# A retention and bilinear-FFN kernel on one core: small filler products at the start, and one pair's stretch moved by four products

## The chip, the cores and the metric

The kernel runs on one core of a Trainium2 chip. The metric is the time of one execution on the device, in microseconds (us). Lower is better. Before the change the median of 7 runs is 329.95 us, with runs from 329.38 to 330.68 us.

The engines are named as in the profile: PE multiplies matrices (PEld is its weight load), DVE and ACT work on vectors, POOL is the general one, and SP issues DMAs. A product is one matrix multiplication instruction. Each is preceded by a weight load of its own, which is an instruction too.

## The reference

There are two layers, the first feeding the second. `q`, `k` and `v` have 8 batches, 8 heads, 576 positions and 64 features; 4608 tokens in all.

```python
def _attn_ref(q, k, v):
    scale = 1.0 / np.sqrt(D_)
    scores = scale * np.matmul(q, k.transpose(0, 1, 3, 2))
    gamma = 1.0 - 2.0 ** (-5.0 - np.arange(H, dtype=np.float32))
    rel = pos[:, None] - pos[None, :]
    Dmat = np.where(rel >= 0, gamma[:, None, None] ** rel[None, :, :], 0.0)
    ret = scores * Dmat[None, :, :, :]
    return np.matmul(ret, v).astype(np.float32)

def _moe_ref(x, w_a, w_b, w_out):      # x is 4608 x 512
    a = x @ w_a                        # 512 x 1536
    b = x @ w_b                        # 512 x 1536
    return (a * b @ w_out).astype(np.float32)
```

The output has 4608 x 512 numbers in float32. The kernel multiplies in bf16.

## The kernel before

**The bulk of the work.** The second layer is computed in blocks of tokens: 512, 256, 256, and then 512 each (`ffn_block`). In a block there are 12 groups F of 128 columns. For each, four products make `pa` (line 728) and four make `pb` (line 743). ACT casts `pa` to `ha` (line 736), and DVE multiplies `ha` with `pb` into `hT` (line 748). After the 12 groups each 128 tokens get 12 products `po` (line 762), which are copied to `osb` and stored. The tiles `pa`, `pb`, `po`, and others of the first layer share four PSUM buffers (`ps_ffn`, tag `ab`).

**The first layer.** Retention is computed in chunks of 64 positions with a running state. The first 768 tokens are done in small steps at the beginning and inside the first block (`score_step`, `state_step`, `output_step`). From token 768 on the tokens are taken in pairs of 128, numbered n (pair 3 is the first, `FIRST`). A pair's work on PE consists of products of 64 x 64 x 64, a quarter of the array each:

- `from_states` (line 613): up to 32 products of states and queries, into `o`;
- `keyed` (line 530): 32 products of keys and values, into `kv`;
- `matched` (line 587): 32 products of keys and queries, into `sc`;
- `from_keys` (line 626): 32 products of scores and values, added into `o`.

`stretch(into, outof)` issues `from_states` for pair `outof`, `keyed` and `matched` for pair `into`, and `from_keys` for `outof`, one after the other. With all four parts it is 128 products and 128 weight loads, hence 256 instructions of PE. Where a state is known to be zero some products are left out: the stretch for pairs 5 and 4 has 240 instructions.

**What follows a stretch on the other engines.** The stretch appends small pieces of work to a list, `later`. One piece is taken off (`pop`) after each `hT`, and at some other points. For pair 5 the six pieces are: two times two sums of `kv` (DVE, line 550); two scalings of `o` into the next block's `xT` (DVE, line 636); then `convert` with the first half of the masked scores; and `convert_swapped` with the second half. `convert` is two casts by ACT (lines 557 and 561), `convert_swapped` two casts by ACT (line 554). These casts make the states which `from_states` of the same pair loads.

**Order.** The order on each engine is written by hand. `ffn_block` yields after every product with that product's cost (1 for 512 columns, 0.5 for 256). The loop at the end adds the costs up. When the sum reaches the place of the first entry of `todo`, and the work is at an edge between groups, that entry runs. `open_alone(5)` at 266 flushes what is left in `later` and issues `from_states` of pair 5; `close_outputs(5)` at 270 issues its `from_keys`. The third block, of 256 tokens, begins at 216, so each of its groups F costs 4.

**Fillers.** At the start PE has no data yet. `warm(count, n)` issues products of a tile of ones whose results nobody reads. The first call is `warm(8, 512)`. Then come the transposes of the first queries and keys (line 316), which wait for casts by DVE (line 299), and more fillers between the first steps.

## Time and profile before

| What | us |
|---|---|
| Median of 7 runs | 329.95 |
| The profiled execution's own time | 329.64 |
| Its span, first to last instruction | 327.9 |
| PE busy with products | 318.0 |
| PEld busy | 168.8 |
| DVE busy | 162.4 |
| ACT busy | 129.2 |
| POOL busy | 114.8 |
| Idle time of PE that the profile puts to no releaser ("issue") before `po`, in 9 places | 1.7 |
| The same before `pa`, in 6 places | 1.0 |

PE's products: 475 recorded for `pb` with 111.2 us, 451 for `pa` with 106.7 us, 429 for `po` with 94.8 us. Some product records are missing, so the counts are slightly under those of the program (3658 products in all, 3621 recorded).

How to read it: times in the timeline are us from the first instruction. A line gives the start, the time covered, the engine, the line of the kernel, the operation with its tiles, and how many instructions are merged (x). In brackets stands the idle time of that engine just before, and what ended it. "issue" means that nothing in the profile explains it. The end of a product is modelled: products overlap, and a single one of 512 columns is shown with 0.38 us, though one follows the other after 0.216 us. So a short idle time in brackets on PE isn't by itself lost time, and like has to be compared with like.

The page also lists DMA queues. Queue 8 is of the kind "instruction": it fetches the program itself. Queue 1 carries the kernel's loads, stores and transposes that SP issues, queue 0 the weight loads that POOL issues.

### The profile page before, as it was taken

To read this page: it belongs to the slowest core of one execution; us is meant where nothing else is said; L and a number is where in the kernel's file an instruction comes from. 1 tells how busy PE (TensorE), PEld (TensorE's weight loads), DVE (VectorE), ACT (ScalarE), POOL (GpSimd) and SP (SyncE) were. 2 spreads that over 40 slices of the span, in tenths; PEclk is the share of its full clock that TensorE was granted. 3 is DMA by queue.
4 is the path that set the end of the run, shared out by engine and by line. 5 is a ranking of instruction groups with operands and counts; after the bars stand their busy time and mean duration, and the time that the engine had idled before them with its cause. 6 is when DMAs were issued, how large, how long until landed. Compare 5 with 4: busy or idle time off the path is not lost.

```text
span 327.9 us, 8698 instructions
## 1 busy us (share of the span) xinstructions
PE 318.0 (97%) x3621; PEld 168.8 (51%) x3658; DVE 162.4 (50%) x291; ACT 129.2 (39%) x277; POOL 114.8 (35%) x146
## 2 busy tenths in 40 slices
PE   7999999999999999999999999999999999999995
PEld 3764467868544554545454545454445444444443
DVE  5744445666536673845274626562556245314421
ACT  6835743553445424533244324442333233213321
POOL 3870069820957067455074205270520000000000
PEclk9999999999999999999999999999999999999999
DMA  7999999999999999994799068935750510031013
GB/s 210 253 186 207 254 231 223 189 216 205 218 220 227 177 212 235 220 217 105 171 216 194 34 159 193 199 97 138 166 115 24 139 35 0 2 96 34 1 32 96
DMA packets 143175, 50.37 MB, mean 154 GB/s; under 512 B 124576, under 2 KB 138656, under 8 KB 143136
## 3 DMA queue, kind: packets, MB, share of 16 engines
q1 hardware_dynamic: 138384, 45.10, 64.6%
q0 software_dynamic: 4752, 4.72, 8.9%
q8 instruction: 28, 0.46, 0.6%
q14 instruction: 11, 0.09, 0.1%
HBM read 37.75 MB, written 9.44 MB: 144 GB/s over the span
## 4 chain that ended last, share of the span: by engine, by line
PE 94%; issue 1%; DMA 1%; DVE 1%; ACT 1%; SPq 0%; ACTq 0%; DVEq 0%
PE pb L743 28%; PE po L762 28%; PE pa L728 27%; PE o L613 2%; PE o L626 2%; DMA vf<-in_v_dram 1%; PE sc L587 1%; PE kv L530 1%; PE kv L360 1%; PE tp L316 1%; PE pa L705 1%; PE o L421 1%; PE sc L331 1%; PE w L792 0%; PE o L405 0%
## 5 line engine op out<-in xcount | busy, mean ns | idle before, releaser
L748 DVE TENSOR_TENSOR hT<-ha,pb 128x512 bf16<-128x512 bf16 (+1 forms) x120 | 75.9, 634 | 98.8 <-PE pb L743 93.3
L736 ACT CAST ha<-pa 128x512 bf16<-128x512 f32 (+1 forms) x120 | 64.9, 544 | 120.1 <-PE pa L728 115.1
L743 PE MATMUL pb<-xT,wb_sb 128*128 128x512 bf16 (+1 forms) x475 | 111.2, 357 | 0.4
L728 PE MATMUL pa<-xT,wa_sb 128*128 128x512 bf16 (+1 forms) x451 | 106.7, 356 | 1.5 <-issue 1.0
L762 PE MATMUL po<-wo_sb,hT 128*128 128x512 bf16 (+1 forms) x429 | 94.8, 373 | 2.1 <-issue 1.7
L743 PEld LDWEIGHTS <-wb_sb 128*128 128x128 bf16 x480 | 47.0, 98 | 46.5 <-issue 0.3
L728 PEld LDWEIGHTS <-wa_sb 128*128 128x128 bf16 x468 | 44.9, 98 | 44.2 <-issue 0.2
L762 PEld LDWEIGHTS <-hT 128*128 128x128 bf16 x444 | 42.3, 98 | 46.9 <-issue 0.3
L464 POOL CAST qkb<-qf 64x1024 bf16<-64x1024 f32 x15 | 15.5, 1031 | 83.3 <-DMA qf<-in_q_dram 83.2
L469 POOL TENSOR_TENSOR vb<-vf,vs 128x1024 bf16<-128x1024 f32 x15 | 28.5, 1903 | 10.4 <-DMA vf<-in_v_dram 5.1
L779 DVE COPY osb<-po 128x512 f32<-128x512 f32 (+1 forms) x16 | 10.8, 675 | 39.3 <-PE po L762 39.3
L777 ACT COPY osb<-po 128x512 f32<-128x512 f32 x20 | 11.7, 587 | 44.3 <-PE po L762 44.3
L636 DVE TENSOR_TENSOR xT<-o,qs 128x512 bf16<-128x512 f32 x30 | 19.5, 683 | 4.4 <-PE o L626 4.4
L550 DVE TENSOR_TENSOR sums<-kv,sums 128x256 f32<-128x256 f32 x46 | 19.5, 423 | 2.8 <-PE kv L530 0.8
L596 DVE TENSOR_TENSOR sT<-sc,mask 128x512 bf16<-128x512 f32 x30 | 19.6, 683 | 0.0
L468 POOL CAST qkb<-kf 64x512 bf16<-64x512 f32 x30 | 17.6, 616 | 0.8
L468 POOL CAST qkb<-qf 64x512 bf16<-64x512 f32 x30 | 17.7, 616 | 0.6
L464 POOL CAST qkb<-kf 64x1024 bf16<-64x1024 f32 x15 | 15.5, 1037 | 6.5 <-DMA kf<-in_k_dram 6.0
L554 ACT CAST states<-sums 64x512 bf16<-64x512 f32 x26 | 16.1, 618 | 0.3
L299 POOL CAST qkb<-kf 128x512 bf16<-128x512 f32 x5 | 3.1, 616 | 18.7 <-DMA kf<-in_k_dram 18.7
L792 PE MATMUL w<-ones 128*128 128x256 bf16 (+1 forms) x34 | 7.4, 346 | 1.5 <-DVE ones L197 1.5
L653 ACT COPY fence<-o 128x2 f32<-128x2 f32 x15 | 2.4, 161 | 15.8 <-PE o L613 15.8
(83 smaller groups left out, 163.3 us busy)
## 6 DMA issues: line engine op xcount, KB each, us to landing
qf<-in_q_dram SPq DMA_DIRECT2D x32, 256.0 KB, 4.7
kf<-in_k_dram SPq DMA_DIRECT2D x32, 256.0 KB, 5.2
vf<-in_v_dram SPq DMA_DIRECT2D x32, 256.0 KB, 5.1
out_dram<-osb SPq DMA_DIRECT2D x25, 256.0 KB, 2.1
out_dram<-osb SPq DMA_DIRECT2D x22, 128.0 KB, 2.7
wo_sb<-in_moe_w_out_dram POOLq DMA_DIRECT2D x3, 512.0 KB, 16.5
qf<-in_q_dram SPq DMA_DIRECT2D x8, 128.0 KB, 3.3
kf<-in_k_dram SPq DMA_DIRECT2D x8, 128.0 KB, 3.5
```

Of the source, the lines that this page charges most:

```text
L464: nc.gpsimd.tensor_copy(qkb[0:64, w], t[0:64])
L468: nc.gpsimd.tensor_copy(to[:, :, 1 - r], fro[:, :, r])
L469: nc.gpsimd.tensor_tensor(vb.rearrange("p (k h d) -> p k h d", k=2, h=H), vf.rearrange("p (k h d) -> p k h d", k=2, h=H), vs2[:, 2 if n in ...
L550: nc.vector.tensor_tensor(sums[:, i], own, prev, op=ALU.add)
L554: nc.scalar.copy(to(half(1 - r)), fro(half(r)))
L596: nc.vector.tensor_tensor(sT[:, on].rearrange("p c k s -> p (c k) s"), sc[:, on].rearrange("p c k s -> p (c k) s"), mask3.unsqueeze(1).to_ ...
L636: nc.vector.tensor_tensor(x_of(t0, 128).rearrange("p c (a s) -> p c a s", a=2), o[:, :, :, kp].rearrange("p a c s -> p c a s"), qs[:, :, s ...
L728: nc.tensor.matmul(pa[:, 0:n], wa_sb[:, c, fs], xT[:, c], start=(c == 0), stop=(c == NC - 1))
L736: nc.scalar.copy(ha[:, 0:n], pa[:, 0:n])
L743: nc.tensor.matmul(pb[:, 0:n], wb_sb[:, c, fs], xT[:, c], start=(c == 0), stop=(c == NC - 1))
L748: nc.vector.tensor_tensor(hT[:, F, 0:n], has[F][:, 0:n], pb[:, 0:n], op=ALU.mult)
L762: nc.tensor.matmul(po[:, 0:width], hT[:, F, u * 128:(u + 1) * 128], wo_sb[:, F, cols], start=(F == 0), stop=(F == NF - 1))
```

## The change

Two things change. The first `warm(8, 512)` becomes three calls of a new function and `warm(5, 512)`. The new function `warm_quads(16)` issues 16 products of 64 x 64 x 64 on the ones, by turns on the upper left and lower right quarter of the array; each call takes a tile of the four shared PSUM buffers. So three products of 512 columns (6 instructions of PE with their weight loads) are replaced by 48 small ones (96 instructions). The number of PE's instructions in the program goes from 7317 to 7407, counting from the branch at the start on.

In `todo` the stretch for pairs 5 and 4 goes from 236 to 240, one group F further on in the third block. The places of the entries around it stay.

```diff
+    def warm_quads(count):
+
+        w = ps_ffn.tile([128, 512], FP32, tag="ab", name="w4")
+        for i in range(count):
+            r = i % 2
+            nc.tensor.matmul(w[half(r), 0:64], ones[half(r), 0:64],
+                             ones[half(r), 0:64], start=True, stop=True)
+
     W1, W2 = 128 * WCOLS[0], 128 * (WCOLS[0] + WCOLS[1])
     vector, pool_ = nc.vector, nc.gpsimd
-    warm(8, 512)
+    for _ in range(3):
+        warm_quads(16)
+    warm(5, 512)
     make_qs(qs_o, 0, 0, 512)
...
     todo += [(170, stretch, (3, None)), (197, stretch, (4, 3)),
-             (236, stretch, (5, 4)), (266, open_alone, (5,)),
+             (240, stretch, (5, 4)), (266, open_alone, (5,)),
              (270, close_outputs, (5,)), (336, stretch, (6, None)),
```

## Prediction

> **What bounds the kernel now.** I read the page first, for the bound.

> ```profile
> span 327.9 us, 8698 instructions
> PE   7999999999999999999999999999999999999995
> PE 94%; issue 1%; DMA 1%; DVE 1%; ACT 1%; SPq 0%; ACTq 0%; DVEq 0%
> q8 instruction: 28, 0.46, 0.6%
> ```

> PE is 94% of the chain of waits and busy in every slice but the ends. After the opening an idle moment of PE is lost time, and nothing else is. The last line is the resource that the change speaks of: 28 packets of 16 KB on queue 8 carry instructions. Next I searched the timeline of PE for idle moments that no semaphore explains. After each dense stretch of 64x64 products PE shows 0.16 us; one place shows more. First the usual exit, then the odd one:

> ```profile
> 119.31 0.33 PEld L762 LDWEIGHTS <-hT 128*128 128x128 bf16 x3
> 119.55 0.38 PE L762 MATMUL po<-wo_sb,hT 128*128 128x512 bf16 x1 [0.16 <-issue]
> ...
> 149.01 0.33 PEld L762 LDWEIGHTS <-hT 128*128 128x128 bf16 x3 [0.28 <-issue]
> 149.24 0.38 PE L762 MATMUL po<-wo_sb,hT 128*128 128x512 bf16 x1 [0.39 <-issue]
> ```

> The timing: the packets of queue 8 start at 56.49, 63.11 and 83.34 us; by the trace PE executes 1205, 1461 and 2229 (block starts) at 55.47, 62.51 and 83.30. So among 256-column products a fetch starts 0.04 to 1.02 us after PE reaches the boundary that triggers it (mean 0.55). A packet takes 0.9 to 1.5 us, mostly 1.25. The one before the odd place ran from 146.18 to 147.51, and PE went on at 149.01: usable 1.5 us after its end.

> [...] The trace agrees: 28 packets of 16 KB, for 28 boundaries among 7317 instructions. [...] Here the trace's clock record reads full from 4.28 us, 2.8 us after the first product; products before that lie 0.43 us apart, later 0.216.

> **The change part by part.**

> *Quarter-array products.* Three products of 512 columns at the half clock go: 3 x 0.427 = 1.28 us. 48 of 64x64x64 come. At full clock the trace shows such products at 10 ns each where four quadrants alternate (128 in 1.23 us, the stretches) and 24 ns where two column halves share their rows (16 in 0.38 us, L360). Two diagonal quarters lie between; twice that at half clock is 20 to 48 ns, so 1.0 to 2.3 us. I take 1.28, no difference. A longer row is covered: the transposes behind the fillers wait for DVE anyway,

> ```profile
> 5.16 0.40 PE L316 MATMUL tp<-identity,qkb 128*128 128x128 bf16 x4 [0.17 <-DVE qkb L299]
> ```

> and the five remaining products shrink to 0.216 us each once the clock is open. With 2.3 us the fillers end at 5.1 instead of 4.6 us, the second transposes start 0.2 later, and the next wait (0.19 us for ACT's vb before L360 at 7.12) takes that up. Cost 0; at most 0.2.

> *Ninety instructions more in front* (96 less 6). Every boundary falls 90 instructions earlier in the work. The odd stretch then has a boundary 91 ahead of it and one in the middle: -0.23 us. I laid the new boundaries over all dense stretches. Next to the one below, the closest is the stretch at old 4958: boundaries 3 instructions ahead of it and 13 behind. Among 512-column products a fetch starts ahead of PE's arrival (146.18 against 147.52), so its block is usable some 1.5 us after arrival, and there PE needs it only after 0.3 + 1.25 + 0.2 + 1.4 = 3.1 us: no stall. In the opening each block lasts over 6 us.

> The one is pair 5's stretch. It keeps 240 instructions and starts at 1991; boundaries are at 1973 and 2229. So 18 ordinary instructions and 238 of the 240 form one block, and only the last load and product belong to the next.

> ```profile
> 75.88 0.26 PEld L613 LDWEIGHTS <-states 64*64 64x64 bf16 x20 [0.21 <-issue]
> 77.11 0.33 PEld L728 LDWEIGHTS <-wa_sb 128*128 128x128 bf16 x4
> ```

> PE reaches 1973 at 75.57 (now instruction 1883). Fetch starts at 75.57 + 0.55 = 76.1, ends at 77.35, is usable at 78.85; with the ends of the ranges 78.1 to 79.45. The stretch starts 8 products of 256 columns later, 75.88 + 0.87 = 76.75, and its last load comes 1.1 us on, at 77.85. Stall 1.0 us (0.25 to 1.6; 0 if blocks are usable earlier than my one case says). Nothing takes it up: DVE's sums for this pair stand behind the next hT, which needs the next pb, so the 0.6 us that PE then loses over PSUM buffers (78.2 to 79.9) come again.

> *Pair 5's stretch four on* (236 to 240: eight 256-column products, one pa and pb). Left in place it would meet the same boundaries. But the move has its own price: the states for `open_alone(5)`, which stays at 266.

> ```profile
> 81.86 0.37 ACT L736 CAST ha<-pa 128x256 bf16<-128x256 f32 x1 [0.50 <-PE pa L728]
> 82.26 0.41 ACT L557 CAST states<-sums 128x256 bf16<-128x256 f32 x1
> 82.57 0.40 ACT L561 CAST left_states<-sums 128x256 bf16<-128x256 f32 x1
> 82.88 0.36 ACT L736 CAST ha<-pa 128x256 bf16<-128x256 f32 x1
> 83.27 1.25 ACT L554 CAST states<-sums 64x512 bf16<-64x512 f32 x2
> 84.42 0.36 ACT L736 CAST ha<-pa 128x256 bf16<-128x256 f32 x1
> ...
> 84.80 0.44 PE L613 MATMUL o<-qkT,states 64*64 64x64 bf16 x32
> ```

> ACT turns the sums into states as the fifth and sixth things popped after the stretch. It ends at 83.27 + 1.25 = 84.52 and PE loads them at 84.80: 0.28 us in hand. After the move the same pops come one pa and pb later: ACT casts ha at 82.73, and the chain of 2.66 us behind it ends at 85.39. PE's work up to L613 is only reordered, so it is there at 84.80 still, and waits until about 85.44: +0.64 us (0 to 0.7). Behind the waiting load stand all of PE's products; nothing later gives it back. ACT's last ha moves ahead of the states, which helps one hT that is not due. A stall inside the stretch moves both sides and doesn't shorten this wait. SP, POOL and the DMA issues keep their order.

> Sum: 0 - 0.23 + 1.0 + 0.64 = +1.41 us. Against the profiled execution: span 327.9 to 329.3, its time 329.64 to 331.05. The median shown is 329.95, 0.31 above that execution, so 331.4.

> **Rivals.**

> Block in time, states late: if the sequencer runs further ahead than I read, or a block is usable soon after its packet ends, the stall falls away: -0.23 + 0.64 = +0.41, 330.35. For it: my 1.5 us come from one place. Against it: at that place nothing else explains the load.

> Not slower, both covered: if PE also arrives at L613 0.64 us later relative to ACT, or ACT's pops come earlier than I place them, only the 0.23 remains: 329.7. It decides once ACT's chain has 0.64 us of reserve more than the 0.28 seen. ACT's start at 81.86 was set by PE, which speaks against.

> Faster: the opening is fetched late now and earlier afterwards. From 14.4 to 17.5 us the dense steps show ten gaps of 0.09 us; were these fetches, 0.9 us would go, with the 0.23: 328.8. It needs all of them to be fetches. Against it: the same 0.09 stands at nearly every entry of a later stretch.

> Clock late: [...] Fillers would end at 4.9 us, [...] the L360 group ends at about 8.6 instead of 8.1: +0.5, with the rest +1.9, 331.9. Nothing in the trace shows such products at half clock.

> **How the numbers follow.** Stall and states both: 0.50. States alone: 0.22. Neither: 0.11. Opening faster: 0.11. Clock late on top: 0.06. 0.2% of the time, 0.66 us, is about what a measurement here can tell from no change. Slower by more than that are the first and the last case and 0.04 of the second (+0.41, near the bound): 0.60. Same: the rest of the second and the third, 0.29. Faster: the fourth, 0.11. The range takes in both smaller cases and the long end of the stall (1.6 instead of 1.0, with 0.2 in the opening): 329.6 to 332.2. The likeliest case alone, with a stall of 0.25 to 1.6, is 330.6 to 332.0.

> **What would show it.** The gap at 149 falls from 0.39 to 0.16 us. Pair 5's last L626 product comes about 1 us after the others, with no semaphore to name. L613 near 86 us waits for ACT's L554, some 0.6 us. Queue 8 has 29 packets. The first transposes still end by 5.4 us. If pair 5's stretch takes 1.23 us as before, my block timing is wrong; if L613 doesn't wait, my ACT chain is.

## The result, and the profile after

The kernel takes 331.84 us after the change (median of 26 runs, 330.37 to 333.05), against 330.19 before (61 runs, 329.25 to 333.43). The ratio is 1.0045, with a 95% interval of 1.0033 to 1.0058. That is 1.5 us slower (1.1 to 1.9). Medians here and below are of all runs, and ratios leave out the three slowest of quads96, which ran at a granted clock of 0.989 to 0.995. The profiled execution took 331.57 us, with a span of 329.9; before it was 329.64 and 327.9.

The page after the change, first the span, PE's busy tenths over 40 slices, the engines' shares of the chain of waits, and the queue of instructions:

```profile
span 329.9 us, 8790 instructions
PE   7899999999999999999999999999999999999995
PE 92%; DMA 2%; SPq 2%; issue 2%; ACT 1%; DVE 1%; ACTq 0%; DVEq 0%
q8 instruction: 29, 0.48, 0.6%
```

PE is the bound as before, so the 2.0 us of span must be time in which PE stands or runs at the low clock of the opening (0.427 us for a product of 512 columns there, 0.216 later, in the kernel before). Queue 8 carries 29 packets instead of 28, for 7407 instructions of PE instead of 7317. By the weight loads that have begun when each packet starts, its packets start 251 instructions of PE apart on average in both traces. The 256 instructions that I count to a block, and the edges counted with them here and below, are an estimate that these numbers fit. The chain of waits now has DMA and SP at 2% each: its first part runs through loads of q in the opening.

To place the 2.0 us I split the span at the first product of L705, which begins the first block of the second layer, and at the last `po`. I call the stretch between them the body.

| | before | after | difference |
|---|---|---|---|
| Start of the first L705 | 17.51 | 18.43 | +0.92 |
| Body: from there to the start of the last `po` | 306.63 | 307.65 | +1.02 |
| From there to the end | 3.79 | 3.78 | -0.01 |

The table of PE's waits by releaser (in total, times, longest) names three waits of this kernel that the one before does not have:

```profile
PE tp L316 <- ACT qkb L299: 0.6, 1, 0.6
PE o L613 <- ACT states L554: 0.4, 1, 0.4
PE o L626 <- ACT fence L653: 0.3, 1, 0.3
```

The first stands in the opening, the other two in the body. The second was expected. In the timeline (start, time covered, in brackets the idle time before and what ended it):

```profile
85.22 1.25 ACT L554 CAST states<-sums 64x512 bf16<-64x512 f32 x2
...
85.88 0.10 PEld L613 LDWEIGHTS <-states 64*64 64x64 bf16 x1 [0.42 <-DVE hT L748]
86.52 0.33 PEld L613 LDWEIGHTS <-states 64*64 64x64 bf16 x31 [0.53 <-ACT states L554]
86.52 0.44 PE L613 MATMUL o<-qkT,states 64*64 64x64 bf16 x31 [0.42 <-ACT states L554]
```

One load goes through at 85.88, and the other 31 wait until ACT's cast ends. From load to load that is 0.64 us, of which I count 0.61 as lost.

The place where I had put the largest loss shows a small one. These are PE's weight loads at the end of pair 5's stretch and behind it:

```profile
78.52 0.36 PEld L626 LDWEIGHTS <-vb 64*64 64x64 bf16 x32
78.92 0.11 PEld L728 LDWEIGHTS <-wa_sb 128*128 128x128 bf16 x2
79.19 0.20 PEld L728 LDWEIGHTS <-wa_sb 128*128 128x128 bf16 x2 [0.15 <-issue]
```

The stretch itself runs through. Two loads behind it PE stands for 0.15 us with no releaser. The stretch at 150 us, whose exit was late before, now leaves with the usual gap:

```profile
150.66 0.33 PEld L762 LDWEIGHTS <-hT 128*128 128x128 bf16 x3
...
150.89 0.38 PE L762 MATMUL po<-wo_sb,hT 128*128 128x512 bf16 x1 [0.16 <-issue]
```

The third wait is one I had not seen coming. `from_keys` (L626) waits for a tiny copy by ACT, the `fence` of line 653, at 235.65. First the kernel before at the same point of the work, then the kernel after:

```profile
233.71 0.16 ACT L653 COPY fence<-o 128x2 f32<-128x2 f32 x1 [0.66 <-PE o L613]
233.92 0.45 PE L626 MATMUL o<-sT,vb 64*64 64x64 bf16 x32
```

```profile
235.65 0.16 ACT L653 COPY fence<-o 128x2 f32<-128x2 f32 x1 [0.94 <-PE o L613]
235.86 0.45 PE L626 MATMUL o<-sT,vb 64*64 64x64 bf16 x32 [0.34 <-ACT fence L653]
```

ACT was idle in both cases and waited for the same product of PE, but the copy starts 0.28 us later. The first product of L626 starts 0.53 us after the one ahead of it, where it was 0.25 before: 0.28 us lost. The same happens at 120.62, where part of it is hidden: 0.18 us lost.

So the body's difference closes: 0.61 (states) + 0.15 (late block) + 0.28 + 0.18 (fences) - 0.23 (the gap at 149 us) = 0.99, against 1.02 measured.

In the opening, the first transposes of step 3 wait for ACT's cast of q, and that waits for the load. Before:

```profile
12.94 0.62 ACT L299 CAST qkb<-qf 128x512 bf16<-128x512 f32 x1
```

And after, in ACT's and in PE's timeline:

```profile
13.87 0.62 ACT L299 CAST qkb<-qf 128x512 bf16<-128x512 f32 x1 [0.92 <-DMA qf<-in_q_dram]
```

```profile
14.54 0.62 PE L316 MATMUL tp<-identity,qkb 128*128 128x128 bf16 x8 [0.59 <-ACT qkb L299]
```

SP issued that load 0.37 us earlier than before (6.96 instead of 7.33), yet it landed 0.93 later (13.85 instead of 12.92). Whether this belongs to the change or to this one execution is a question for the experiments.

### The profile page after: what moved, and what is told of

The parts are those of the page before. It is cut to its first block, busy times and chain, and to the rows that moved or that the text cites. A ratio compares the mean times of both kernels' runs of the same rounds, so it can differ in the third digit from the quotient of the medians.

```text
span 329.9 us, 8790 instructions
## 1 busy us (share of the span) xinstructions
PE 319.2 (97%) x3665; PEld 170.5 (52%) x3703; DVE 162.4 (49%) x291; ACT 129.4 (39%) x277; POOL 114.8 (35%) x146
## 4 chain that ended last, share of the span: by engine, by line
PE 92%; DMA 2%; SPq 2%; issue 2%; ACT 1%; DVE 1%; ACTq 0%; DVEq 0%
PE pb L743 28%; PE po L762 28%; PE pa L728 27%; DMA qf<-in_q_dram 2%; SPq L153 2%; PE o L613 2%; PE o L626 2%; PE sc L587 1%; PE kv L530 1%; PE pa L705 1%; PE kv L360 1%; PE o L421 1%; PE tp L316 0%; ACT states L554 0%; PE o L405 0%
## 5 line engine op out<-in xcount | busy, mean ns | idle before, releaser
L736 ACT CAST ha<-pa 128x512 bf16<-128x512 f32 (+1 forms) x120 | 64.9, 544 | 120.8 <-PE pa L728 115.9
L728 PE MATMUL pa<-xT,wa_sb 128*128 128x512 bf16 (+1 forms) x451 | 106.9, 356 | 1.5 <-issue 1.0
L762 PE MATMUL po<-wo_sb,hT 128*128 128x512 bf16 (+1 forms) x429 | 94.8, 373 | 1.8 <-issue 1.4
L728 PEld LDWEIGHTS <-wa_sb 128*128 128x128 bf16 x468 | 44.9, 98 | 44.4 <-issue 0.4
L762 PEld LDWEIGHTS <-hT 128*128 128x128 bf16 x444 | 42.3, 98 | 46.7
L554 ACT CAST states<-sums 64x512 bf16<-64x512 f32 x26 | 16.1, 618 | 0.3
L299 POOL CAST qkb<-kf 128x512 bf16<-128x512 f32 x5 | 3.1, 616 | 19.0 <-DMA kf<-in_k_dram 19.0
L339 DVE TENSOR_TENSOR sT<-sc,mask_s 128x1024 bf16<-128x1024 f32 x6 | 7.3, 1222 | 3.1 <-PE sc L331 3.1
L653 ACT COPY fence<-o 128x2 f32<-128x2 f32 x15 | 2.4, 161 | 16.4 <-PE o L613 13.6
```

Of the source, the lines that this page charges most:

```text
L554: nc.scalar.copy(to(half(1 - r)), fro(half(r)))
L728: nc.tensor.matmul(pa[:, 0:n], wa_sb[:, c, fs], xT[:, c], start=(c == 0), stop=(c == NC - 1))
L736: nc.scalar.copy(ha[:, 0:n], pa[:, 0:n])
L762: nc.tensor.matmul(po[:, 0:width], hT[:, F, u * 128:(u + 1) * 128], wo_sb[:, F, cols], start=(F == 0), stop=(F == NF - 1))
```

## The experiments

Twelve kernels ran, each in five rounds beside the kernel before. "Ratio" is to the kernel before on the same chip; 0.001 is 0.33 us. Where a wait for `qkT` (a transposed tile that DMA makes) is given, its size is from start to start: from the last product of L530 to the first of L587, less what the kernel before takes there. The bracket of the same line is 0.1 to 0.2 us smaller, as the modelled end of a product hides a part. Three questions: what does each half of the change do, are the body's rows the right ones, and what in the opening costs time?

### Each half alone: quads_only and move_only

quads_only has the small fillers and leaves the stretch at 236:

```diff
+    for _ in range(3):
+        warm_quads(16)
+    warm(5, 512)
-    warm(8, 512)
```

> The filler part alone: 48 quarter-array products in front, pair 5's stretch back at 236. My theory (states late 0.6 us, blocks of instructions late at pair 5's stretch, minus the gap at 149): the states are in time again, so 0.6 us less than the changed kernel. What is left is the block, 0.15 to 1.0 us, and -0.23: 329.9 to 331.0. Rival (the opening carries the loss: small products keep the clock low until 7.5 us): the whole +1.5 stays, 331.7.

Measured: 331.26 us, ratio 1.0034 (1.0018 to 1.0051), so 1.1 us slower: above my range and below the rival's 331.7. The wait for states and the late fences are absent, and so is the late exit at 149 us. The block behind pair 5's stretch is 0.14 us late, not 1. The body is 307.87, and 1.57 of it is one wait for `qkT`:

```profile
133.37 0.45 PE L587 MATMUL sc<-qkT 64*64 64x64 bf16 x32 [1.40 <-DMA qkT<-qkb]
```

Without it the body would be 306.30, 0.33 less than before: 0.23 of it is the late exit, and smaller steps, none above 0.13, more than make up the 0.14 of the block. So in this half alone the body but for that wait is no slower, and still the kernel is. The time must be ahead of the body or in waits such as this one.

move_only has the old fillers and the stretch at 240:

```diff
-             (236, stretch, (5, 4)), (266, open_alone, (5,)),
+             (240, stretch, (5, 4)), (266, open_alone, (5,)),
```

> The move alone: stretch at 240, the old eight fillers. My theory: L613 waits for ACT's states some 0.6 us near 86 us, the gap of 0.39 at 149 stays, no block of instructions is late: +0.6, 330.8. Rival (opening): no change, 330.2.

Measured: 331.31 us, ratio 1.0022 (1.0007 to 1.0038). The median is 0.5 above my 330.8; the ratio gives 0.7 us where I had 0.6, but of other parts. The wait for states is there (0.61), and both late fences (0.46). So the fences belong to the move, not to the fillers. The exit near 149 us is later than ever, as the program keeps its boundary inside the old stretch:

```profile
150.14 0.98 PEld L762 LDWEIGHTS <-hT 128*128 128x128 bf16 x6 [0.98 <-issue]
150.14 1.25 PE L762 MATMUL po<-wo_sb,hT 128*128 128x512 bf16 x5 [0.87 <-issue]
```

PE is without a weight load for 0.98 us here. The packet of queue 8 ran from 147.33 to 148.64, so the block was usable 1.5 us after its end. The body is 308.63; 0.34 of that is a wait for `qkT` near 67 us.

### The states: after_open270 and move270

`open_alone(5)` and `close_outputs(5)` follow the stretch by four products too, so the distance between the sums and their use is the old one. In after_open270 this is done to the changed kernel, in move270 to move_only:

```diff
-             (240, stretch, (5, 4)), (266, open_alone, (5,)),
-             (270, close_outputs, (5,)), (336, stretch, (6, None)),
+             (240, stretch, (5, 4)), (270, open_alone, (5,)),
+             (274, close_outputs, (5,)), (336, stretch, (6, None)),
```

> The changed kernel with the two entries behind the stretch also moved by four: open_alone(5) at 270, close_outputs(5) at 274. My theory: L613 no longer waits for ACT's states, 0.6 us less than the changed kernel: 331.1. Rival (opening): as the changed kernel, 331.7.

Measured: 330.97 us, ratio 1.0024 (1.0007 to 1.0041), 0.7 us less than the changed kernel by the two ratios, whose intervals overlap. The casts and the load that waited for them, now in order:

```profile
84.22 1.25 ACT L554 CAST states<-sums 64x512 bf16<-64x512 f32 x2
...
85.75 0.33 PEld L613 LDWEIGHTS <-states 64*64 64x64 bf16 x32 [0.42 <-DVE sT L596]
```

The load begins 0.28 us after the casts end, the same reserve as in the kernel before. The fences stay late, and the block at pair 5's stretch 0.13 us. The body is 306.88, against 307.65: 0.77 less, where the states wait was 0.61.

> The old fillers, the stretch at 240, and pair 5's state pass and closing each four products later too (270 and 274). Theory 'two late waits in the body': the 0.6 us that L613 waits for L554's states is gone, the two late fences (near 119 and 235, 0.46 together) stay, and so does the late block at 150 us: 330.6 to 330.9 by median, body about 308.0 less any wait for qkT. Rival, the moved stretch costs something of its own that the trace gives no row: the time stays at move_only's 331.2 to 331.4.

Measured: 330.99 us, ratio 1.0014 (0.9999 to 1.0029). No wait for states. The late fences stay, and the late exit at 150 us too (0.48 instead of 0.23). The body is 307.30. The rows give 306.63 + 0.46 + 0.25 = 307.34, so my 308.0 was too high: it counted a wait for `qkT` that this execution does not have. The median lies between my 330.6 to 330.9 and the rival's 331.2.

### The fences: open270_act2, move_act2 and move270_act2

Why would ACT, idle, start a copy 0.28 us late? The copy is preceded by a wait instruction of its own. In the kernels with the moved stretch, at the two late places, the copy follows that wait by 0.32 us instead of 0.04. The two copies have the numbers 191 and 319 among the instructions that the trace records on ACT: 128 apart. The kernels with the moved stretch have 408 of them, the others 406. If ACT's own instructions come in blocks, which is a guess here, the edge fell between wait and copy. Queue 14, the other queue of instructions, carries packets of 8 KB, half the size of queue 8's; the traces do not say which engine each is for. To test it, two tiny copies on ACT are put ahead of the body:

```diff
     load_pair(FIRST + 2, (Q, K))
+    for _ in range(2):
+        nc.scalar.copy(fence, biasq[:, 0:1].to_broadcast([128, 2]))
```

> The changed kernel with open_alone(5) at 270 and close_outputs(5) at 274, and two tiny copies more on ACT before the second layer begins. In the three moved kernels seen so far ACT's fence copy (L653) comes 0.28 us late at 119-121 and 234-236 us, 128 ACT instructions apart, which costs PE 0.46 in all. Theory: these are boundaries of ACT's own blocks of instructions, which two extra instructions push off the fence: both delays go, 0.4 less than after_open270, 330.6. Rival (the fence is late because the moved stretch changes what ACT does there): both stay, 331.0.

Measured: 331.64 us, ratio 1.0031 (1.0011 to 1.0050). In the trace both fences are on time:

```profile
234.15 0.16 ACT L653 COPY fence<-o 128x2 f32<-128x2 f32 x1 [0.38 <-PE o L613]
234.35 0.45 PE L626 MATMUL o<-sT,vb 64*64 64x64 bf16 x32
```

The body is 306.42, 0.46 less than after_open270's. But the time did not fall: the first L705 is at 18.15 instead of 17.52, and the median is higher than the rival's 331.0. That the delay hangs on the number of ACT's instructions ahead is shown by the trace; that a fetch is behind it fits, but no row names one. The gain in time is not shown.

> The old fillers, the stretch at 240 and two tiny copies on ACT ahead of the body, so that ACT's own blocks of instructions change two instructions earlier in the program. Theory: the fences near 119 and 235 us are no longer late (0.28 each at ACT, 0.46 of PE's time), while the states wait of 0.6 stays: 330.7 to 331.0. Rival, the late fences hide in what PE would have waited anyway: 331.2 to 331.4.

Measured: 330.83 us, ratio 1.0009 (0.9991 to 1.0026). The fences near 120 and 235 us are on time, and the wait for states stays with 0.61. The late exit at 150 us is gone as well, which I had not expected: PE came to that place later, and goes on at 150.66 after 0.17 us with no releaser. A wait for `qkT` (0.8 us) took its place.

> The old fillers, the stretch at 240, the state pass and the closing at 270 and 274, and the two tiny copies on ACT. Theory: both costs of the move in the body are gone and the time is before's but for the late block at 150 us (0.5 more than before's at 149): 330.3 to 330.8, with no wait of L613 for L554 and no late fence. Rival, the move has a cost that neither row holds: above 331.0.

Measured: 331.00 us, ratio 1.0018 (1.0000 to 1.0036), above my 330.8 and just at the edge of the rival. The trace has no wait for states, no late fence and no late exit. The body is 306.42, 0.21 less than before. All of this profile's loss lies ahead of it: the first L705 is at 19.29, and most of that is one wait, listed by releaser as

```profile
PE kv L360 <- ACT vb L307: 0.9, 1, 0.9
```

which again ends with a load that came late. So in this execution the body's costs are those in the rows, and the move has no other there.

### The small products, or the place of the blocks? n128, full90, merge16, quads_late, quads96

n128 cuts the eight first fillers into 32 full-array products of 128 columns, 48 instructions more, with the stretch at 236:

```diff
-    warm(8, 512)
+    warm(32, 128)
```

> No small products: the first eight fillers of 512 columns become 32 of 128 columns on the whole array, 48 instructions more, stretch at 236. Block boundaries lie clear of all stretches, the gap at 149 is gone. Theory O: the clock opens at 4.3 to 5 us as before, nothing is lost in the opening: 330.0 to 330.2. Rival (any rise of the number of instructions in front costs in the opening): 330.7 or more.

Measured: 330.14 us, ratio 0.9993 (0.9978 to 1.0007). The late exit at 149 us is gone, the body is 306.77 with two waits for `qkT`, 0.66 together. Here more instructions in front cost nothing.

merge16 goes the other way: four later groups `warm(4, 256)` become `warm(2, 512)`, 16 instructions fewer.

> The kernel before with fewer instructions instead of more: four groups of four fillers of 256 columns become two of 512 each, 16 instructions less, stretch at 236. The block boundary that lay at the end of the stretch at 149 us moves 16 instructions on. Theory: gap at 149 falls from 0.39 to 0.16, nothing else moves: 330.0 to 330.3. Rival (the gap belongs to that stretch, not to the boundary): 0.39 stays.

Measured: 330.54 us, ratio 1.0007 (0.9984 to 1.0029), above my 330.3 by median but no change by ratio. The exit that was late is on time (149.03 follows 148.63 directly), and the body is 306.42. A boundary 16 instructions later does as well as one 90 earlier: the gap moves with the boundary. In exchange PE stands for 0.46 us in the opening at 16.34, with no releaser, 1.4 us after the first packet of queue 8 ended (13.76 + 1.14).

quads_late keeps the first fillers and puts 52 small products in place of seven later ones, 90 instructions more:

```diff
-    warm(5, 256)
+    warm_quads(22, 2, 256)
...
-    warm(4, 256)
+    warm_quads(30)
```

> The same 90 instructions more, but after the clock is open: the eight fillers of 512 columns stay, and seven later fillers of 256 columns become 52 quarter-array products (22 in place of three before the second score step's successor, 30 in place of four before the transposes of step 3). Stretch at 236. My theory: as quads_only, since the block boundaries are the same: 329.9 to 331.0. Rival (opening): the clock opens at 4.3 us as before, and the time is that of the kernel before or 0.2 better: 330.0 to 330.2.

Measured: 331.66 us, ratio 1.0040 (1.0022 to 1.0058), above my range and the rival's. The opening has a stall of this kind too, larger:

```profile
15.39 0.25 PE L421 MATMUL o<-sT,vb 64*64 64x128 bf16 x4 [0.81 <-issue]
```

0.97 us are lost there, and 0.40 behind pair 5's stretch. The first packet ended at 13.82, 1.6 us before PE went on.

quads96 has twice the small products (96 for six of 512 columns), 180 instructions more.

> The filler part doubled, stretch at 236: 96 quarter-array products for six of the eight. 180 instructions more, which puts no block boundary just ahead of any stretch, so no block of instructions is late in the body and the gap at 149 is gone (-0.23). Theory O (small products don't count for the clock; [...] and the opening pays): first score step later than with 48 (after 7 us), time 0.5 or more above quads_only: 331.5 to 332.5. Rival B (the filler part costs through late blocks at pair 5's stretch): 329.9 to 330.2.

Measured: 331.99 us, ratio 1.0043 (1.0019 to 1.0066). The record of PE's clock reads full from 4.4 us, as in the kernel before, so small products do not keep the clock from opening. The second score step begins at 10.07, where it was 10.08. So the time lies in theory O's range by luck: what O said of the clock did not happen. In its profile `qkT` costs 2.6 us at 70.89 and 0.3 more later, and the first L705 starts at 18.63.

full90 takes up what n128 left open. It has exactly the 90 more instructions of the change, all full-array, in the opening:

```diff
-    warm(8, 512)
+    warm(32, 128)
...
-    warm(4, 256)
+    warm(8, 128)
...
-    warm(3, 256)
+    warm(6, 128)
...
-    warm(5, 256)
+    warm(10, 128)
```

(and two more groups of four, and one of one, cut in the same way).

> No quarter-array products and the stretch at 236, but exactly the 90 more PE instructions that the change adds, all as full-array products (the eight openers as 32 of 128 columns, and six later filler groups cut into twice as many products of 128 columns), so the block boundaries of the body stand where they stand with the quads in front and the stretch at 236 (331.26). Theory B, the extra cost of the quads alone comes from where the block boundaries and the fetches fall, in the opening among others: 330.9 to 331.4, first L705 at 18.2 or later or a fetch before 11 us with a step's load behind it landing late. Theory Q, it comes from the quarter-array products themselves, [...]: 330.1 to 330.5, first L705 by 17.8. Both: no gap of 0.39 at 149 us, and no states wait.

Measured: 331.38 us, ratio 1.0019 (1.0002 to 1.0036). The median is inside theory B's range and outside theory Q's; but the kernel before stood at 330.58 beside it, and the 0.6 us of the ratio lie between the two theories. The first L705 is at 18.28 and the first packet starts at 10.11 us. The largest single loss in its profile is this wait, 1.9 us from start to start:

```profile
79.38 0.45 PE L587 MATMUL sc<-qkT 64*64 64x64 bf16 x32 [1.73 <-DMA qkT<-qkb]
```

So a kernel without any quarter-array filler is slower as well, though by hardly more than its interval. The small products by themselves seem not to be needed for a loss; the ratios' intervals are too wide to say that they add nothing.

### What the rows leave over: the opening and the late tiles

One profile cannot tell what the change does to the opening. Three kernels share the opening of the kernel before, instruction for instruction on PE and ACT, and their profiles begin L705 at different times:

```profile
17.51 2.35 PE L705 MATMUL pa<-xT,wa_sb 128*128 128x256 bf16 x20
```

```profile
16.91 2.78 PE L705 MATMUL pa<-xT,wa_sb 128*128 128x256 bf16 x24
```

```profile
18.32 1.47 PE L705 MATMUL pa<-xT,wa_sb 128*128 128x256 bf16 x12
```

These are before, move_only and move270. Part of the spread of 1.4 us I put to a block of instructions arriving late: in move270 PE stands at L421 until 16.36, with no releaser, and loses 0.7 us there; the first packet had ended 1.5 us before. In the kernel before the same packet ran 0.74 us earlier, and no such gap is seen. Three kernels with the small fillers in front begin at 18.43 (after), 17.29 (quads_only) and 17.52 (after_open270). The +0.92 of the result is therefore within what one execution differs from another.

The times of all runs say more. For each kernel I take the ratio's microseconds and subtract what its body gained or lost in the profile, waits for `qkT` left out of the body, since they come and go. What remains is whatever the body's other rows don't hold: the opening, and the waits for `qkT`.

| kernels | what remains, us |
|---|---|
| 90 or more instructions more ahead of the dense steps: after, after_open270, full90, open270_act2, quads_only, quads96 | 0.5, 0.6, 0.9, 1.3, 1.4, 1.8; mean 1.1 |
| others: move_only, move270, move_act2, n128, merge16, move270_act2 | -1.0, 0.0, 0.0, 0.3, 0.5, 0.8; mean 0.1 |
| quads_late, with a stall of 0.97 in the opening | 1.2 |

Each ratio is uncertain by 0.4 to 0.8 us, and each body is that of one execution, so single values are not worth much; the first two groups differ by 1.0. The profiles point to the late tiles more than to the opening. The first L705 starts at 18.05 us on average in the first group and at 17.97 in the second. The waits for `qkT` beyond those of the kernel before take 1.1 us on average in the first group (0.0, 0.1, 2.2, 0.1, 1.6 and 2.9 in the order of the table) and 0.3 in the second (0.3, 0.2, 0.8, 0.7, 0.1 and 0.0). That is six single executions on each side, with three of them making the difference, so it is a pointer and no proof.

Why `qkT` would come late there is not settled. In the first group the first packet of queue 8 starts at 7.2 to 10.9 us, in the midst of the loads of the first steps; in the kernel before it starts at 12.99. A collision with those loads, and a chain from loads over casts and transposes to `qkT`, would fit the late load of after and the late `qkT` of quads_only, quads96 and full90. But n128's first packet starts at 10.84 and costs nothing by ratio, and 0.9 and 0.5 us of late loads occur in move270_act2 and open270_act2 too. This stays an argument.

No version beat the kernel before by more than a measurement can tell; n128 at 0.9993 came nearest.

## Why the prediction was right, and where

The forecast was 331.4 us and +1.41; measured were 331.84 and +1.5. The sum came out well, its terms less so, and that the total is so close is luck.

- **States, +0.64: right.** 0.61 was lost, at the place and to the releaser named, and moving the two later entries by the same four products takes it away in all four kernels in which it was done (after_open270, move270, open270_act2, move270_act2).
- **The gap at 149 us, -0.23: right.** It goes whenever the boundary leaves the stretch (quads_only, n128, merge16), and varies when the boundary remains: larger in move_only and move270, absent in the two kernels with act2, in which PE came to that place later.
- **Pair 5's late block, +1.0: the term that was mis-sized; it measured 0.15.** The place was right but for some six instructions, the step was wrong in two ways. I let the fetch start 0.55 us after PE reached instruction 1973, the mean of three cases. It started 0.33 us before (76.23, PE there at 76.56 by the trace). In five other kernels with this boundary it started from 0.13 before to 0.84 after, and the latest of these, quads_late, has the longest stall, 0.40. And PE missed the block only two loads behind the stretch, 0.27 us later than I had it. The packet took 1.50 us rather than 1.25, which gave 0.25 back. Together: 1.0 - 0.88 - 0.27 + 0.25 = 0.1. The time from a packet's end to its use was right: 1.46 us against my 1.5.
- **The small fillers themselves, 0 (at most 0.2).** 48 of them took 1.43 us, 30 ns each, for 1.28 replaced, and the first transposes ran from 5.05 to 6.1 instead of ending by 5.4, as the clock opened at 7.45 us (fillers of 256 columns follow each other after 0.21 us at 6.1 and after 0.11 at 7.6). The rival of a late clock came true in the trace of after; its moment and its +0.5 us were assumed, not shown by the kernel before. It came without its price: the second score step began at 10.08, exactly as before, so PE had caught up by then. Other kernels with the same fillers opened at 4.4 to 6.2 us, so a late clock isn't what the small products do. In the fourteen traces here it opened at 4.28 to 7.45 us, 2.8 to 5.9 after the first product; what sets the moment is not shown.
- **Ninety instructions in the opening, 0: the reason was wrong.** I said each block there lasts over 6 us and looked no further. The first two packets of the kernel before start at 12.99 and 16.85 us, 3.9 apart, and PE stood there for 0.46 to 0.97 us with no releaser in merge16, move270 and quads_late. The trace of after has no such stall. Kernels with 90 instructions more have some 1.0 us more that the body's rows don't hold, cause open.
- **ACT, nothing: wrong.** I counted instruction blocks for PE only. The move changes the number of ACT's instructions by two, and two fences, 128 of ACT's recorded instructions apart, came late, as they would at edges of ACT's blocks: +0.46.

So the misses cancelled: 0.85 too much for the block, 0.46 and an uncertain part of a microsecond too little elsewhere. The rows also account for the profiled execution better than for the times. open270_act2 has none of the body's losses and is still 1.0 us slower than the kernel before, and the fillers alone (quads_only) cost 1.1 us, where my terms give 0.8 through a block that measured 0.14.

## What to carry to other kernels

When a change adds or removes instructions, count the block edges on every engine that PE waits for, and on all of the stream; one edge in dense work cost from nothing to 0.97 us here, and which ones are hit changes with every edit. When a stage is moved, move what depends on it by the same amount, or work out the reserve: here it was 0.28 us. For effects below 1 us split the span at landmarks and compare the parts, and take one execution's opening for a sample, not for a measurement.

## What the runs showed that I had not expected

- Where PE stood with no releaser at such an edge, it went on 1.3 to 1.7 us after the 16 KB packet had ended (1.31 in quads_late behind the stretch, 1.46 in after, 1.50 in move_only, 1.67 in quads_only), so 2.3 to 3.0 us after it had begun. The time lost was 0.13 to 0.97 us. In the kernel before one place stands out for 28 packets, the 0.39 us at 149 us; in its table of waits PE has no other without a releaser above 0.2. Such stands came at a stretch, where 256 instructions of PE pass in 1.23 us, and in the dense steps of the opening.
- A tiny copy on ACT, for which PE waits, came 0.28 us late at two places, 128 of ACT's recorded instructions apart, in all four kernels that move the stretch and add nothing on ACT; two more instructions on ACT, ahead of the body, made it punctual in all three kernels that have them. Elsewhere the same copy follows its wait in 0.04 us. That these are edges of ACT's own blocks is inferred from this.
- The same instructions in the opening end 1.4 us apart from one execution to another, which is more than most of the edits here are worth.
